# Stacking transfers of units 1 to 4 issued from two queues in turn

## The chip, the cores and the metric

The kernel runs on one core of a Trainium2 chip. The metric is the device time of one execution in microseconds (us). The core's engines are TensorE (PE; its weight loads are listed apart as PEld), VectorE (DVE), ScalarE (ACT), GpSimd (POOL) and SyncE (SP). Each executes its own instructions in order and waits on semaphores for the others. SyncE and ScalarE issue the transfers, which 16 DMA engines carry out.

## The reference

A linear recurrence with a complex diagonal decay per batch, head and key channel, followed by a bilinear feed-forward. Shapes: batch 4, 8 heads, 768 tokens, head width 48; the feed-forward is 384 to 1536 to 384.

```python
mag = sqrt(a_re*a_re + a_im*a_im)
scale = minimum(mag, 0.999) / (mag + 1e-6)
ar, ai = a_re*scale, a_im*scale                       # decay of each channel d at each token
for t in range(768):                                  # S_re, S_im: 48 x 48 per batch and head
    S_re, S_im = (ar[t]*S_re - ai[t]*S_im + outer(k[t], v[t]),
                  ar[t]*S_im + ai[t]*S_re)
    y[t] = q[t] @ S_re
x = y with the heads side by side                     # 3072 x 384
out = ((x @ w_a) * (x @ w_b)) @ w_out                 # 3072 x 384
```

## The kernel before

The work is cut into 12 **units** (`NU`): two pairs of batches, six chunks of 128 tokens each, so a unit covers 256 tokens (`TOK`, two batches of 128) for all eight heads. Three kinds of work run beside each other:

- **Prep** of a unit (`prep`, mostly VectorE with ScalarE): from the decays it forms running products z over the chunk, and multiplies queries and keys in the tile `qk` by them (L312 is the last of it, two multiplies for each unit from the third on, four for units 0 and 1, which are treated in two halves). Its first steps are the two multiplies of L214, the negation L216 on ScalarE, and then pairs of L230 and L236 on VectorE. Inside the prep of unit u runs `scale` for unit u+1 (L181 to L196), which turns raw decays into scale factors on ScalarE and VectorE.
- **Attention** of a unit (`attn`, mostly TensorE): scores by head (L385), a mask multiply on VectorE (L388), outputs (L425), transposes of the keys (L396, copied by ScalarE in L400) and the state update (L442). ScalarE (L429) and VectorE (L434) turn its result into the pair `xh`, `xl`.
- **Feed-forward** of a unit: twelve blocks f, each with `gemm1` (18 matmuls, L494), a copy and a product by ScalarE and VectorE (L502 to L505), and `gemm2` (6 matmuls, L512), which runs two blocks behind. ScalarE copies the two results of a unit (L651) and issues their transfers to memory (L652).

Between prep and attention stands the **stacking**. `qk` holds query and key rows of all heads in three groups of 128 partitions, and the tile `stk` holds, for each head, 96 partitions in which real and imaginary rows are stacked. `stack(u)` moves the one to the other by transfers from SBUF to SBUF: one for each head, two for heads 2 and 5, whose rows cross a group's border, so ten in all (L352). In the kernel before, SyncE issues all of them. For units 0 and 1 (`u < EARLY`) the first half of the columns is stacked earlier, in the middle of prep, by a call with explicit columns; the later call moves the other half.

The main loop goes over units w. While the feed-forward of unit w runs, the attention of unit w+1 is laid between its blocks, and prep for later units goes on. In the program text, at block 11 (10 for later w), the rest of the attention and of prep(w+2) is followed by stack(w+2), by the load of the next `qk` (L340, SyncE), and then by prep(w+3). For w = 0, stack(1) comes at block 4, in the middle of the conversion of the weights (L137 to L152), and is followed by eight extra matmuls (L681).

The order of instructions on each engine is set by a planner when the kernel is built: it goes through the program with its own estimate of every instruction's time, and at each moment takes for an engine the ready instruction that comes first in the program text. Some instructions are given a priority far ahead of their place (`high_priority`: the copies and products of the feed-forward, and the attention's steps on VectorE and ScalarE). From w+1 = 5 (`LED`) on, TensorE's order is the program's own, and the planner orders the other engines alone. On the chip, the engines then follow these orders, whatever the times.

Of the kernel before, what the change touches and what calls it, by code (L numbers as in the profile page):

```python
# [49 lines left out]
LED = 5  # L50
# [20 lines left out]
def tile_kernel(ctx: ExitStack, tc: tile.TileContext, a_d, qk_d, v_d, w_d, qn_d, kn_d, vn_d, an_d, out_d):  # L71
    nc = tc.nc
    vec, act, pe, sync = nc.vector, nc.scalar, nc.tensor, nc.sync
# [35 lines left out]
    stk = const.tile([128, H, RUN], F32, name="stk")  # L109
    nc.gpsimd.memset(stk[KS:128], 0.0)  # L110
    qk = const.tile([128, NJ, 2, RUN], F32, name="qk")
# [88 lines left out]
    def rescaled(c):  # L200
        return c % 2 == 1 and c + 1 < NCH

    def prep(u):
# [113 lines left out]
        if u < EARLY:  # L317
            for k in range(2):
                times_p(k, 0, 1)
            stack(u, slice(0, TOK))  # L320
# [20 lines left out]

    def stack(u, cols=None):
        n = RUN if rescaled(u % NCH) else 2 * TOK
        if cols is None:
            cols = slice(TOK if u < EARLY else 0, n)
        for h in range(H):
            r0 = h * D
            while r0 < (h + 1) * D:
                j, p = divmod(r0, 128)
                m = min((h + 1) * D - r0, 128 - p)  # L350
                d0 = 2 * (r0 - h * D)
                sync.dma_start(out=stk[d0:d0 + 2 * m, h, cols], in_=qk[p:p + m, j, :, cols])  # L352
                r0 += m


# [276 lines left out]
    drain(scale(0, a_tiles[0], z_first))  # L632
    drain(prep(0))
    stack(0)
    load_qk(1)
    p1 = prep(1)
# [19 lines left out]
    for w in range(NU):  # L656
# [15 lines left out]
        for f in range(NF):  # L672
            if w == 0:
                next(ws, None)
                drain(p1, P1_F)
                if f == P1_AT:
                    drain(p1)
                    stack(1)
                    for i in range(WARM):
                        wp = ps_m.tile([128, 512], F32, name="pm")  # L680
                        pe.matmul(out=wp[:, 0:TOK], lhsT=ident, rhs=qk[:, i % NJ, 1 - i // NJ % 2, TOK:2 * TOK],  # L681
                                  start=True, stop=True)
                    load_qk(2)
                    pgen = prep(2)
            pend.append((w, f, *gemm1(f, *x_cur), os_))
            if len(pend) > LAG:
                second()
            slot()
            if f == STACK_AT[min(w, 4)]:
                drain(at)  # L690
                if w + 2 < NU:
                    drain(pgen)
                    stack(w + 2)
                if w + 3 < NU:
                    load_qk(w + 3)
                    pgen = prep(w + 3)
            if w > 0:
                drain(pgen, 2400)
# [71 lines left out]
```

## Time and profile before

| | |
|---|---|
| median of 3 runs | 691.67 us (690.39 to 691.81) |
| profiled execution | 692.08 us |
| its span, first to last instruction | 690.4 us |
| mean granted TensorE clock | 0.974 |
| busy: PE, PEld | 647.5 us (94%), 607.9 us (88%) |
| busy: DVE, ACT | 552.1 us (80%), 306.7 us (44%) |
| stacking transfers | 140, of 32 to 193 KB |

The median and the profiled execution are two different readings: a trace explains its own execution. A row of the trace in order of time gives the start from the span's beginning, the length, engine, line of the kernel, operation, what it writes and reads, and in brackets the idle time of its engine just before and what ended it. SPq and ACTq are the queues of SyncE and ScalarE issuing transfers: such a row's length is that of the issue, not of the transfer; the landing is told apart. Rows of the same kind that follow each other are merged, with their count.

### The profile page before, as it was taken

What the parts mean: (1) busy time and instruction counts of PE and PEld (TensorE: products, weight loads), DVE (VectorE), ACT (ScalarE), POOL (GpSimd) and SP (SyncE); (2) the same over time, 40 slices, a digit from 0 to 9 for tenths busy, and PEclk for the clock granted to TensorE, in tenths of its full rate; (3) what the DMA queues carried; (4) which work ended last, traced back from release to release, by engine and by line L of the source; (5) the groups of instructions that cost most, each with busy time, mean ns of one, the idle gap of its engine ahead of it and who ended that gap; (6) DMA issues with size and microseconds to landing.
All of it is one profiled execution on the core that took longest, in us unless ns stands there. A gap on an engine that the chain in (4) does not pass through costs nothing.

```text
span 690.4 us, 14307 instructions
## 1 busy us (share of the span) xinstructions
PE 647.5 (94%) x5854; PEld 607.9 (88%) x5854; DVE 552.1 (80%) x1241; ACT 306.7 (44%) x618; POOL 5.6 (1%) x11
## 2 busy tenths in 40 slices
PE   3647999999999999999999999999999999999996
PEld 1224889899899999999999999999999999999995
DVE  6999899998898979989899898999989963233221
ACT  6347655634634445245353463634542332222221
POOL 3000000000000000000000000000000000000000
PEclk9577999999999999999999999999999999999999
DMA  8983201411414205224151250511410410400000
GB/s 310 402 303 109 80 1 47 139 54 49 137 43 125 87 28 150 62 92 131 32 161 47 84 155 1 166 73 49 121 69 16 112 65 18 107 24 2 24 1 28
DMA packets 32087, 63.93 MB, mean 93 GB/s; under 512 B 3984, under 2 KB 10640, under 8 KB 32016
## 3 DMA queue, kind: packets, MB, share of 16 engines
q1 hardware_dynamic: 28560, 58.23, 27.2%
q10 hardware_dynamic: 3456, 4.72, 1.9%
q8 instruction: 48, 0.79, 0.5%
q14 instruction: 23, 0.19, 0.1%
HBM read 39.32 MB, written 4.72 MB: 64 GB/s over the span
## 4 chain that ended last, share of the span: by engine, by line
PE 59%; DVE 31%; ACT 4%; DMA 2%; issue 2%; SPq 0%; ACTq 0%; DVEq 0%
PE ab L494 28%; PE o L512 13%; PE pm L385 5%; PE xp L425 4%; DVE a_t L292 3%; DVE qk L312 3%; PE pm L442 3%; DVE pr L230 2%; DVE hl L505 2%; DVE h_t L503 2%; PE pm L150 2%; DVE z L297 2%; DVE pb L260 2%; DVE z L236 1%; PE ab L150 1%
## 5 line engine op out<-in xcount | busy, mean ns | idle before, releaser
L494 PE MATMUL ab<-xh,w 128*128 128x256 f32 x1728 | 339.5, 285 | 0.0
L494 PEld LDWEIGHTS ab<-xh,w 128*128 128x128 f32 x1728 | 278.0, 190 | 1.0 <-issue 0.6
L494 PE MATMUL ab<-xl,w 128*128 128x256 f32 x864 | 245.1, 284 | 0.2 <-DVE xl L434 0.2
L494 PEld LDWEIGHTS ab<-xl,w 128*128 128x128 f32 x864 | 164.5, 190 | 1.0 <-DVE xl L434 0.7
L512 PE MATMUL o<-w,hh 128*128 128x384 f32 x576 | 149.5, 338 | 0.5 <-ACT o_sb L651 0.5
L502 ACT COPY h_t<-ab 128x256 f32<-128x256 f32 x144 | 53.3, 370 | 164.0 <-PE ab L494 163.0
L503 DVE TENSOR_TENSOR h_t<-ab,h_t 128x256 f32<-128x256 f32 x144 | 60.7, 421 | 64.8 <-ACT h_t L502 64.5
L504 ACT CAST hh<-h_t 128x256 fp32r<-128x256 f32 x144 | 58.2, 404 | 100.4 <-DVE h_t L503 100.0
L512 PEld LDWEIGHTS o<-w,hh 128*128 128x128 f32 x576 | 97.2, 190 | 1.7 <-ACT o_sb L651 1.1
L512 PE MATMUL o<-w,hl 128*128 128x384 f32 x288 | 97.0, 337 | 0.0
L505 DVE TENSOR_TENSOR hl<-h_t,hh 128x256 fp32r<-128x256 f32 x144 | 60.9, 423 | 21.5 <-ACT hh L504 21.3
L150 PE MATMUL ab<-o_sb,ident 128*128 128x384 f32 x42 | 27.8, 765 | 31.2 <-DVE o_sb L141 31.2
L385 PE MATMUL pm<-stk 128*128 128x128 f32 x384 | 53.5, 280 | 2.2 <-DMA stk<-qk 2.2
L512 PEld LDWEIGHTS o<-w,hl 128*128 128x128 f32 x288 | 54.1, 188 | 0.0
L385 PEld LDWEIGHTS pm<-stk 128*128 128x128 f32 x384 | 47.9, 191 | 6.9 <-issue 5.2
L230 DVE TENSOR_TENSOR pr<-z 128x384 f32<-128x384 f32 (+1 forms) x91 | 47.3, 527 | 2.7 <-ACT z L216 0.9
L150 PEld LDWEIGHTS ab<-o_sb,ident 128*128 128x128 f32 x42 | 10.0, 281 | 40.8 <-DVE o_sb L141 31.0
L292 DVE TENSOR_TENSOR a_t<-z,b_t 128x768 f32<-128x768 f32 x48 | 44.9, 956 | 0.0
L312 DVE TENSOR_TENSOR qk<-qk,z 128x1536 f32<-128x1536 f32 (+1 forms) x28 | 42.7, 1524 | 0.0
L425 PE MATMUL xp<-am,v_t 128*32 128x128 f32 x768 | 39.7, 276 | 0.7 <-DVE am L388 0.6
L388 DVE TENSOR_TENSOR am<-pm,mask 128x512 f32<-128x512 f32 x48 | 32.9, 689 | 4.0 <-PE pm L385 4.0
L425 PE MATMUL xp<-stk,u 128*32 128x128 f32 x640 | 32.7, 273 | 0.0
(106 smaller groups left out, 751.9 us busy)
## 6 DMA issues: line engine op xcount, KB each, us to landing
w<-in_dram SPq DMA_DIRECT2D x36, 384.0 KB, 8.0
qk<-in_dram SPq DMA_DIRECT2D x12, 768.0 KB, 4.9
a_t<-in_dram SPq DMA_DIRECT2D x11, 768.0 KB, 4.3
stk<-qk SPq DMA_DIRECT2D x42, 192.0 KB, 3.3
v_t<-in_dram SPq DMA_DIRECT2D x24, 256.0 KB, 2.7
out_dram<-o_sb ACTq DMA_DIRECT2D x24, 192.0 KB, 2.2
stk<-qk SPq DMA_DIRECT2D x18, 192.8 KB, 3.2
stk<-qk SPq DMA_DIRECT2D x14, 128.0 KB, 3.1
```

Of the source, the lines that this page charges most:

```text
L150: pe.matmul(out=lp[:, 0:n], lhsT=ident, rhs=t, start=True, stop=False)
L230: vec.tensor_tensor(out=pr[:, :, :, o:o + n], in0=view(zz, W + at_(i) + 2 * o, [[W, 2], [-W, 2], [2, n]]), in1=tok(slice(1, 3), i - 1, o, ...
L292: vec.tensor_tensor(out=pz[:, s].rearrange("p (j b e) -> p j b e", j=SUB // 2, e=2), in0=zb[:, 1 + s], in1=view(bb, (1 + k - s) * NB, [[0, ...
L312: vec.tensor_tensor(out=qk4[:, :, k, x0:x1], in0=qk4[:, :, 1, x0:x1], in1=z[:, k].rearrange("p (j t) -> p j t", j=NJ).unsqueeze(2).broadca ...
L385: pe.matmul(out=sp[:, h4], lhsT=stk[:, h, ks], rhs=stk[:, h, qs], start=True, stop=True)
L425: pe.matmul(out=xp[qd * 32:(qd + 1) * 32, ti], lhsT=l, rhs=rr, start=st, stop=sp_, tile_position=(0, qd * 32), skip_group_check=True)
L494: pe.matmul(out=ab[:, m * TOK:(m + 1) * TOK], lhsT=r(w_ab(f, part, m * NJ + i)), rhs=r(xt[:, i, :]), start=n == 0, stop=n == 8)
L502: act.copy(out=h_t, in_=ab[:, 0:TOK])
L503: vec.tensor_tensor(out=h_t, in0=ab[:, TOK:2 * TOK], in1=h_t, op=ALU.mult)
L504: act.copy(out=r(hh), in_=h_t)
L505: vec.tensor_tensor(out=r(hl), in0=h_t, in1=hh, op=ALU.subtract)
L512: pe.matmul(out=os_[tt][:, 0:DM], lhsT=r(ht[:, ts]), rhs=r(w_t[f, 2][:, part, :]), start=(f == 0 and n == 0), stop=(f == NF - 1 and n == 2))
```

## The change

`stack` gets a list of queues. For the call without explicit columns, and for units 1 to 4 (`0 < u < LED`), the list is SyncE and ScalarE, and the ten transfers are issued by them in turn: SyncE takes the first, third and so on, ScalarE the second, fourth and so on. For all other units, and for the early halves of units 0 and 1, SyncE issues all of them as before. The transfers themselves are the same.

```diff
     def stack(u, cols=None):
         n = RUN if rescaled(u % NCH) else 2 * TOK
+        queues = [sync]
         if cols is None:
             cols = slice(TOK if u < EARLY else 0, n)
+            if 0 < u < LED:
+                queues = [sync, act]
+        k = 0
         for h in range(H):
             r0 = h * D
             while r0 < (h + 1) * D:
                 j, p = divmod(r0, 128)
                 m = min((h + 1) * D - r0, 128 - p)
                 d0 = 2 * (r0 - h * D)
-                sync.dma_start(out=stk[d0:d0 + 2 * m, h, cols], in_=qk[p:p + m, j, :, cols])
+                queues[k % len(queues)].dma_start(out=stk[d0:d0 + 2 * m, h, cols], in_=qk[p:p + m, j, :, cols])
+                k += 1
                 r0 += m
```

## The prediction

> **What bounds the kernel now.** I read the page first, then busy time by stage, then the chain of work that ended last, and last the order of time around each stacking. The page gives the span; the profiled execution took 692.08 us in all, so 1.68 us lie around the span, and the median of the runs is 691.67 us, 0.41 us below this execution. A difference worked out inside the span is therefore added to 691.67.
>
> ```profile
> span 690.4 us, 14307 instructions
> ```
>
> Busy time by stretch (microseconds of the stretch, then busy time of PE, PEld, DVE, ACT):
>
> ```profile
> 85.00:170.00 85.00, 84.94 (x695) 78.33 (x694) 80.10 (x187) 43.65 (x90) 0.00 (x0) 1.00 0.19 55
> 170.00:262.00 92.00, 89.58 (x896) 85.75 (x895) 80.98 (x182) 43.26 (x82) 0.00 (x0) 1.00 0.28 85
> 262.00:391.00 129.00, 129.00 (x1254) 125.87 (x1253) 119.14 (x257) 61.24 (x119) 0.00 (x0) 1.00 0.31 91
> 391.00:556.00 165.00, 164.45 (x1592) 160.86 (x1591) 153.58 (x344) 75.86 (x151) 0.00 (x0) 1.00 0.31 93
> ```
>
> From 85 to 556 us TensorE is busy throughout, at a granted clock of 1.00, but for 2.4 us in the second row and 0.55 in the last. The second row holds the stackings of units 2 and 3. The chain there runs through the first stacking transfer of each unit to the score matmuls:
>
> ```profile
> 171.17 3.29 DMA stk<-qk
> ...
> 217.76 3.36 DMA stk<-qk
> ```
>
> TensorE in order of time (start, length, idle time before it and its releaser) shows the first scores of units 1 to 5 and its one later wait:
>
> ```profile
> 128.76 0.38 PE L385 MATMUL pm<-stk 128*128 128x128 f32 x2
> 174.59 0.46 PE L385 MATMUL pm<-stk 128*128 128x128 f32 x2 [1.57 <-DMA stk<-qk]
> 221.25 0.46 PE L385 MATMUL pm<-stk 128*128 128x128 f32 x2 [0.68 <-DMA stk<-qk]
> 268.69 0.85 PE L385 MATMUL pm<-stk 128*128 128x128 f32 x4
> 322.46 1.95 PE L385 MATMUL pm<-stk 128*128 128x128 f32 x16
> 555.46 0.61 PE L512 MATMUL o<-w,hh 128*128 128x384 f32 x2 [0.55 <-ACT o_sb L651]
> ```
>
> Units 2 and 3 stall TensorE for 1.57 and 0.68 us, together 2.25 us, each time for the **first** of the ten transfers and for none of the other nine. That sum is all that this change can take out of TensorE's path.
>
> **The change part by part.** Each of the four stackings has ten transfers (eight heads, of which heads 2 and 5 are cut in two). Of these five stay with SyncE and five go to ScalarE: 20 issues moved, nothing added or removed.
>
> *What the second queue saves.* SyncE's rows of units 1 to 5, each with ten issues:
>
> ```profile
> 122.32 6.34 SPq L352 DMA_DIRECT2D stk<-qk  x10
> 171.17 6.63 SPq L352 DMA_DIRECT2D stk<-qk  x10
> 217.76 6.67 SPq L352 DMA_DIRECT2D stk<-qk  x10
> 265.09 6.67 SPq L352 DMA_DIRECT2D stk<-qk  x10
> 308.88 6.67 SPq L352 DMA_DIRECT2D stk<-qk  x10
> ```
>
> Ten issues in 6.3 to 6.7 us are 0.64 to 0.67 us each with the gap. With five on each engine the issuing ends after 3.3 us instead of 6.7, if the two engines issue side by side. The data don't follow at that pace. For unit 3 the whole burst, and four microseconds in its middle (the last two numbers are the busy share of the 16 DMA engines and GB/s):
>
> ```profile
> 217.80:227.20 9.40, 8.72 (x69) 8.30 (x68) 8.36 (x18) 7.15 (x13) 0.00 (x0) 1.00 0.63 168
> 221.00:225.00 4.00, 3.75 (x30) 3.78 (x31) 3.03 (x7) 2.64 (x6) 0.00 (x0) 1.00 0.81 220
> ```
>
> The burst is 9.40 x 0.63 = 5.9 us of work for all 16 engines, and in its middle they are 81% busy already. A whole head is an eighth of that, 0.74 us. The first lands after 3.36 us, so its data start to move about 2.6 us after the issue, and the last can't land before 2.6 + 5.9 = 8.5 us, against 9.4 now: **0.9 us earlier for the last head, nothing for the first**. The first may land later, as the neighbour's packets now run beside its own: between 0 and 0.74 us late. [...]
>
> [...]
>
> For the stall this means: unit 2's 1.57 becomes 1.92. Unit 3's first transfer lands 0.35 later too, but TensorE also arrives 0.35 later, so the loss isn't counted twice. Unit 4 has its first transfer at 265.09 + about 3.3 = 268.4, and TensorE took it at 268.69: 0.3 us of cover, about enough. Unit 1 is transferred from 122.32 on and half its heads' columns were moved earlier; its scores start at 128.76, 6.4 us after the first issue, so its faster landing is worth nothing. **Term one: +0.35 us.** The load of `qk` behind the stacking on SyncE's queue may go out 0.9 us earlier; none of the waits shown above is for it, so it is costed at nothing.
>
> *What the issues cost on ScalarE.* ScalarE executes in order, and a DMA issue holds back what follows. The trace shows it at its own output transfers, and shows what stands where unit 2's five issues will go (171.2 us on):
>
> ```profile
> 204.63 0.34 ACTq L652 DMA_DIRECT2D out_dram<-o_sb  x1
> 205.01 0.41 ACT L504 CAST hh<-h_t 128x256 fp32r<-128x256 f32 x1 [0.41 <-ACT o_sb L651]
> ...
> 171.51 0.41 ACT L504 CAST hh<-h_t 128x256 fp32r<-128x256 f32 x1 [2.08 <-DVE h_t L503]
> 172.38 0.85 ACT L216 ACTIVATE z<-z 128x768 f32<-128x768 f32 x1 [0.46 <-DVE z L214]
> ...
> 126.74 0.85 ACT L216 ACTIVATE z<-z 128x768 f32<-128x768 f32 x1 [0.82 <-DVE z L214]
> ```
>
> At 205 us the cast waited 0.41 us through a 0.34 us issue. A stacking issue has another shape; its nearest row is SyncE's 0.64 us, and five of them are 3.2 us (bounds: 5 x 0.34 = 1.7 and 5 x 0.67 = 3.4; I take 3.2, because the transfers are the very same). In the program text stack(u) comes before prep(u+1), so the planner has reason to put the issues ahead of L216, the negation that opens the next unit's scan, and of L181 after it; the high-priority cast L504 can slip between. L216 then starts at 171.17 + 3.2 + 0.41 = 174.8 at the latest, and 172.38 at the best (issues behind it). VectorE needs it:
>
> ```profile
> 173.85 0.55 DVE L230 TENSOR_TENSOR pr<-z 128x384 f32<-128x384 f32 x1
> ...
> 178.24 0.69 DVE L388 TENSOR_TENSOR am<-pm,mask 128x512 f32<-128x512 f32 x1 [0.78 <-PE pm L385]
> 182.85 0.69 DVE L388 TENSOR_TENSOR am<-pm,mask 128x512 f32<-128x512 f32 x1 [0.53 <-PE pm L385]
> 189.12 0.42 DVE L503 TENSOR_TENSOR h_t<-ab,h_t 128x256 f32<-128x256 f32 x1 [0.90 <-ACT h_t L502]
> ```
>
> L230 would start at 174.8 + 0.85 = 175.7 instead of 173.85: up to 1.8 us late, 0 at best. Behind it VectorE has idle time of 0.78 + 0.53 + 0.90 = 2.2 us before 190 us that could swallow this, but each of those waits is for TensorE, and a mask multiply L388 that comes late on VectorE's queue makes TensorE late in turn. So the net is between 0 and 1.8 us for a unit; I take the middle, 0.9 minus a bit for L504 and L502 that fill part of the hole: **0.8 us**. It counts where the next stacking is waited for: after unit 2 (unit 3's stall) and after unit 3 (unit 4, less its 0.3 us of cover). After unit 4 it doesn't count: unit 5's transfers are issued from 308.88 and its scores come at 322.46, 13.6 us later, against 9.4 us that a burst takes. After unit 1 it doesn't either: L216 comes at 126.74, and the five issues end at 122.32 + 3.2 = 125.5.
>
> **The sum.** TensorE is 0.35 us late after unit 2. Unit 3's data come 0.35 + 0.8 late: 1.15. Unit 4's come 0.35 + 1.6 late with 0.3 covered: 1.65. Past 262 us TensorE has no idle time, so that stays; the 0.55 at 555 us gives no cover, since the chain into it is itself fed by TensorE:
>
> ```profile
> 386.70 0.42 DVE L503 TENSOR_TENSOR h_t<-ab,h_t 128x256 f32<-128x256 f32 x1 [0.93 <-ACT h_t L502]
> ```
>
> Here VectorE waits for a gemm result by way of ScalarE. 692.08 + 1.65 = 693.7 us against the profiled execution, **693.3 us** against the median. Its own range is 692.0 (only term one is left) to 695.3 (1.8 for each of the two units, less 0.3, plus 0.35).
>
> **The rivals.**
>
> *Absorbed.* VectorE's 2.2 us of idle time swallow the late L216, and only term one is left: 691.67 + 0.35 = 692.0 us. For it speaks that those waits really are idle; against it that they end with TensorE's own work.
>
> *Faster: the new plan pulls the scores later.* TensorE's order for units 1 to 4 is the planner's, and it placed unit 2's first score 1.57 us too early. If the planner prices the issues on ScalarE dear, it puts VectorE's chain and the scores later against the gemms; the chip then finds the data landed, and both stalls vanish: 2.25 us. From then on the gain must get past 386.70, where VectorE's idle time for TensorE is 0.93 us, and 555.46, where TensorE already waits 0.55 us for the ScalarE and VectorE chain; so 0.93 is the lower bound of what is kept and 2.25 the upper. With 1.7, nearer the upper bound because that chain has other waits, 690.0 us. It decides as soon as the scores move back by more than L216's lateness.
>
> *Slower still: the two issue streams wait for each other.* At unit 6 two output transfers from ScalarE fell into SyncE's burst. The stacking issues of unit 3 and of unit 6 (min/median/max ns, then us to landing), and all of ScalarE's issues:
>
> ```profile
> L352 SPq DMA_DIRECT2D stk<-qk x10: 585/600/722, 217.8 to 223.8; - x10
> DMA to landing us min/median/max: 2.6/3.2/3.4
> L352 SPq DMA_DIRECT2D stk<-qk x10: 576/596/1596, 351.9 to 359.7; - x10
> DMA to landing us min/median/max: 2.6/3.2/4.8
> L652 ACTq DMA_DIRECT2D out_dram<-o_sb x24: 338/338/473, 151.2 to 684.7; - x24
> ```
>
> The longest issue grew from 722 to 1596 ns and the longest landing from 3.4 to 4.8 us. If the streams take turns, the change doesn't do what it says: nothing is issued sooner, and ScalarE is held for all ten issues, 6.4 us. L216 then starts at 171.17 + 6.4 + 0.41 = 178.0 and L230 at 178.85, 5.0 us late; with 2.2 swallowed that is 2.8 for each of the two units, and 5.6 - 0.3 + 0.35 = 5.65 in all: 697.3 us. It decides as soon as ScalarE's issues take clearly more than 0.64 us each. Against it: the neighbours at unit 6 wrote to HBM, and no issue of ScalarE's took over 473 ns.
>
> [...]
>
> **How the numbers follow.** A measurement of this kernel tells 0.2% from no change, 1.38 us. Chances: the forecast 0.42 (two thirds of it, 0.28, beyond +1.38 us), absorbed 0.20, faster 0.24 (0.22 beyond -1.38 us), slower still 0.14. Slower is 0.28 + 0.14 = 0.42, same 0.14 + 0.20 + 0.02 = 0.36, faster 0.22. The range runs from 689.9 us, 1.8 of the faster rival's 2.25 us, to 697.0 us, just short of the last rival; it leaves out about half of that one and the end of the other.
>
> **What would show it.** Right: ten transfers on two queues with issues side by side, the first landing after 3.3 to 4.1 us, the last some 8.5 us after the first issue; L216 of units 2 to 4 starting two microseconds later against L312's end; VectorE's idle time before L230 up; TensorE's waits for `stk` at units 2 and 3 at or above 1.6 and 0.7 us. Wrong: those waits gone while L216 stays in place, or issues on ScalarE of 0.34 us, or a TensorE wait in a stage past 262 us, where I expect none.

## The result, and the profile after

The changed kernel takes **705.23 us** (median of four runs, 700.73 to 705.85) against 691.52 us for the kernel before (four runs): a ratio of 1.0183, 95% interval 1.0167 to 1.0199, or 13.7 us more. The prediction was 693.3 us. The profiled execution took 705.57 us. One of the four runs, 700.73 us, had a mean granted clock of 0.972 where the others had 0.965 or 0.966; it left no trace. In the rows of the changed kernel the lines of the program have moved down: the stacking L352 is L356, and from there on all stand five further, the scores L385 at L390, the mask multiply L388 at L393, the first gemm L494 at L499, the feed-forward's copy L502 and product L503 at L507 and L508; L214 to L312 are where they were.

The page's span, and busy time by stretch of the changed kernel (same columns and stretches as in the prediction):

```profile
span 703.9 us, 14315 instructions
```

```profile
85.00:170.00 85.00, 84.00 (x688) 77.21 (x687) 79.08 (x185) 42.81 (x89) 0.00 (x0) 1.00 0.18 51
170.00:262.00 92.00, 85.80 (x840) 81.42 (x839) 74.53 (x170) 37.21 (x72) 0.00 (x0) 0.96 0.29 84
262.00:391.00 129.00, 125.05 (x1166) 121.12 (x1165) 111.38 (x233) 61.52 (x116) 0.00 (x0) 0.99 0.31 92
391.00:556.00 165.00, 165.00 (x1634) 161.56 (x1633) 153.62 (x341) 76.27 (x154) 0.00 (x0) 1.00 0.27 78
```

TensorE is idle for 1.00 + 6.20 + 3.95 + 0 = 11.15 us of these 471, where it was 3.03 before: 8.1 us more. And its granted clock, 1.00 everywhere before, is 0.96 over 92 us and 0.99 over 129, about 5 us of full speed. Together that is 13.1 of the 13.5 us by which the span grew. So there are two losses to explain, waits and a lower clock, and the second stood in no case of the prediction.

The waits, in TensorE's order of time, for units 2, 3, 4 and 5 of the changed kernel:

```profile
175.43 0.46 PE L390 MATMUL pm<-stk 128*128 128x128 f32 x2 [1.74 <-DMA stk<-qk]
176.97 0.49 PE L390 MATMUL pm<-stk 128*128 128x128 f32 x2 [1.08 <-DMA stk<-qk]
...
179.42 0.80 PE L390 MATMUL pm<-stk 128*128 128x128 f32 x2 [0.46 <-DMA stk<-qk]
...
227.31 0.46 PE L390 MATMUL pm<-stk 128*128 128x128 f32 x2 [1.28 <-DMA stk<-qk]
229.22 0.79 PE L390 MATMUL pm<-stk 128*128 128x128 f32 x2 [1.45 <-DMA stk<-qk]
...
280.66 0.46 PE L390 MATMUL pm<-stk 128*128 128x128 f32 x2 [0.66 <-DMA stk<-qk]
282.47 0.49 PE L390 MATMUL pm<-stk 128*128 128x128 f32 x2 [1.34 <-DMA stk<-qk]
...
337.63 0.83 PE L390 MATMUL pm<-stk 128*128 128x128 f32 x4 [1.10 <-DMA stk<-qk]
```

Before, TensorE waited once in unit 2 and once in unit 3, for the first head, and not at all in units 4 and 5. Now it waits for the **second** head too, by 1.08, 1.45 and 1.34 us, in unit 4 as well, and by 1.10 us even in unit 5, which SyncE stacks alone as before.

ScalarE in order of time at unit 2, and VectorE behind it:

```profile
171.83 0.60 ACTq L356 DMA_DIRECT2D stk<-qk  x1
172.48 0.41 ACT L509 CAST hh<-h_t 128x256 fp32r<-128x256 f32 x1 [2.39 <-DVE h_t L508]
172.50 1.32 ACTq L356 DMA_DIRECT2D stk<-qk  x1
...
173.95 0.85 ACTq L356 DMA_DIRECT2D stk<-qk  x1
...
177.03 1.24 ACTq L356 DMA_DIRECT2D stk<-qk  x2
178.32 0.84 ACT L216 ACTIVATE z<-z 128x768 f32<-128x768 f32 x1 [3.07 <-DMA stk<-qk]
```

```profile
175.28 0.42 DVE L510 TENSOR_TENSOR hl<-h_t,hh 128x256 fp32r<-128x256 f32 x1 [0.53 <-ACT hh L509]
180.26 0.69 DVE L393 TENSOR_TENSOR am<-pm,mask 128x512 f32<-128x512 f32 x1 [4.55 <-PE pm L390]
180.86 0.55 DVE L230 TENSOR_TENSOR pr<-z 128x384 f32<-128x384 f32 x1
```

The five issues reach from 171.83 to 178.27, 6.4 us, and L216 comes at 178.32 (172.38 before). Between 174.80 and 177.03 ScalarE issues nothing: but for a cast of 0.40 us it waits, and the row of L216 names the landing of a stacking transfer. (The 3.07 us in that row are this wait, from 175.24 on, and the two issues behind it.) The order of ScalarE's instructions as the planner wrote it, with the semaphores that each waits for, shows what for (DMAHW0 to 7 are the eight semaphores on which the transfers of both queues report that they have landed):

```
192 L356 DMA stk<-qk 96x1x512 [waits DMAHW2_49]
193 L509 CAST hh<-h_t 128x256 [waits DVE_49]
194 L356 DMA stk<-qk 64x1x512 [waits DMAHW5_49,DMAHW4_49,DMAHW1_49]
195 L356 DMA stk<-qk 96x1x512 [waits DMAHW6_49]
196 L216 ACTIVATE z<-z 128x768
```

With one queue an issue waits for the transfer eight places ahead, which had landed by then: in unit 2 the first transfer landed at 174.46 and the ninth was issued at 176.55, and SyncE's ten issues of before follow each other within 6.63 us, without a pause. With two, ScalarE's fourth issue waits for transfers that are under way, its own first one among them (DMAHW5), issued 5.2 us earlier and landed at 176.93.

VectorE, for its part, did not wait for L216 in unit 2. It waited 4.55 us for a score, since its new order has the mask multiply L393 ahead of the next unit's L230; before, L230 ran at 173.85, ahead of the mask multiply at 178.24. The two delays lie over each other: L216 ended at 179.16, so even ahead of the mask multiply L230 could have begun only 1.7 us earlier. In unit 3 the held ScalarE shows on VectorE directly. There the feed-forward's copy L507 stood behind a landing wait of ScalarE's issues, and VectorE's product L508 behind the copy:

```profile
230.96 0.37 ACT L507 COPY h_t<-ab 128x256 f32<-128x256 f32 x1 [4.90 <-DMA stk<-qk]
```

```profile
231.37 0.42 DVE L508 TENSOR_TENSOR h_t<-ab,h_t 128x256 f32<-128x256 f32 x1 [4.85 <-ACT h_t L507]
```

Between 165 and 345 us its mask multiplies, before and after, had these waits (busy time and mean ns of one, then the idle time before them and what ended it):

```profile
L388 DVE TENSOR_TENSOR am<-pm,mask 128x512 f32<-128x512 f32 x16 | 11.1, 691 | 2.2 <-PE pm L385 2.2
```

```profile
L393 DVE TENSOR_TENSOR am<-pm,mask 128x512 f32<-128x512 f32 x14 | 9.6, 688 | 13.2 <-PE pm L390 13.2
```

The planner wrote all three orders anew. TensorE's, around unit 2 (h0: the scores of head 0; g5: five feed-forward matmuls), as it was executed:

```
before:  h0 g5 h1 g11 h2 g4 h3 g4 h4
after:   h0 h1 g5 h2 g2 h3 g3 h4
```

The planner now lays heads 0 and 1 directly behind each other, as if two queues delivered two heads at a time. The chip delivered otherwise: TensorE started head 0 at 175.43 and head 1 at 176.97. The stacking transfers of unit 2, before and after (issue time min/median/max in ns, then us from issue to landing):

```profile
L352 SPq DMA_DIRECT2D stk<-qk x10: 592/599/718, 171.2 to 177.2; - x10
...
DMA to landing us min/median/max: 3.0/3.7/4.8
```

```profile
L356 SPq DMA_DIRECT2D stk<-qk x5: 595/767/904, 171.8 to 174.9; - x5
L356 ACTq DMA_DIRECT2D stk<-qk x5: 588/608/1324, 171.8 to 177.7; - x5
...
DMA to landing us min/median/max: 3.5/4.9/6.3
```

A transfer took 1.2 us longer at the median. TensorE could start head 1 at 176.97, 5.15 us after the first issue.

The clock, in two neighbouring stretches of 3.41 us at unit 2 (the column behind POOL's busy time is the granted clock):

```profile
174.56:177.97 3.41, 1.46 (x10) 1.29 (x11) 0.62 (x2) 0.40 (x1) 0.00 (x0) 1.00 0.98 252
177.97:181.38 3.41, 2.95 (x15) 2.66 (x14) 1.12 (x2) 2.31 (x3) 0.00 (x0) 0.50 0.55 129
```

After a stretch in which TensorE was idle for 1.95 of 3.41 us, it ran one stretch at half its clock. The same follows the waits of units 3 and 4, at 229.17 and 283.79 us. A stretch of 3.41 us at half clock does 1.7 us less work: three times 1.7 us.

### The profile page after: what moved, and what is told of

It reads as the page before. It is cut to its first block, busy times and chain, and to the rows that moved or that the text cites. A ratio compares the mean times of both kernels' runs of the same rounds, so it can differ in the third digit from the quotient of the medians.

```text
span 703.9 us, 14315 instructions
## 1 busy us (share of the span) xinstructions
PE 654.8 (93%) x5854; PEld 612.2 (87%) x5854; DVE 551.1 (78%) x1241; ACT 307.3 (44%) x618; POOL 5.6 (1%) x11
## 4 chain that ended last, share of the span: by engine, by line
PE 66%; DVE 19%; DMA 7%; ACT 3%; SPq 3%; issue 1%; ACTq 0%; DVEq 0%
PE ab L499 32%; PE o L517 15%; PE pm L390 6%; PE xp L430 5%; DMA stk<-qk 4%; PE pm L447 3%; DMA w<-in_dram 3%; DVE qk L312 3%; DVE a_t L292 3%; SPq L356 3%; PE pm L401 2%; DVE h_t L508 1%; DVE z L297 1%; DVE hl L510 1%; DVE pb L260 1%
## 5 line engine op out<-in xcount | busy, mean ns | idle before, releaser
L499 PE MATMUL ab<-xh,w 128*128 128x256 f32 x1728 | 341.1, 286 | 0.0
L499 PEld LDWEIGHTS ab<-xh,w 128*128 128x128 f32 x1728 | 279.5, 191 | 1.0 <-issue 0.6
L499 PE MATMUL ab<-xl,w 128*128 128x256 f32 x864 | 245.9, 285 | 0.2 <-DVE xl L439 0.2
L499 PEld LDWEIGHTS ab<-xl,w 128*128 128x128 f32 x864 | 165.3, 191 | 0.8 <-DVE xl L439 0.5
L507 ACT COPY h_t<-ab 128x256 f32<-128x256 f32 x144 | 53.0, 368 | 165.3 <-PE ab L499 159.3
L508 DVE TENSOR_TENSOR h_t<-ab,h_t 128x256 f32<-128x256 f32 x144 | 60.5, 420 | 65.5 <-ACT h_t L507 65.1
L390 PE MATMUL pm<-stk 128*128 128x128 f32 x384 | 56.3, 289 | 9.9 <-DMA stk<-qk 9.9
L390 PEld LDWEIGHTS pm<-stk 128*128 128x128 f32 x384 | 49.6, 196 | 16.4 <-issue 8.5
L230 DVE TENSOR_TENSOR pr<-z 128x384 f32<-128x384 f32 (+1 forms) x91 | 47.3, 527 | 2.8 <-ACT z L216 1.1
L393 DVE TENSOR_TENSOR am<-pm,mask 128x512 f32<-128x512 f32 x48 | 32.7, 687 | 14.9 <-PE pm L390 14.9
L312 DVE TENSOR_TENSOR qk<-qk,z 128x1536 f32<-128x1536 f32 (+1 forms) x28 | 42.7, 1523 | 0.2
```

What stands on the lines that cost most here:

```text
L230: vec.tensor_tensor(out=pr[:, :, :, o:o + n], in0=view(zz, W + at_(i) + 2 * o, [[W, 2], [-W, 2], [2, n]]), in1=tok(slice(1, 3), i - 1, o, ...
L312: vec.tensor_tensor(out=qk4[:, :, k, x0:x1], in0=qk4[:, :, 1, x0:x1], in1=z[:, k].rearrange("p (j t) -> p j t", j=NJ).unsqueeze(2).broadca ...
L390: pe.matmul(out=sp[:, h4], lhsT=stk[:, h, ks], rhs=stk[:, h, qs], start=True, stop=True)
L499: pe.matmul(out=ab[:, m * TOK:(m + 1) * TOK], lhsT=r(w_ab(f, part, m * NJ + i)), rhs=r(xt[:, i, :]), start=n == 0, stop=n == 8)
L507: act.copy(out=h_t, in_=ab[:, 0:TOK])
L508: vec.tensor_tensor(out=h_t, in0=ab[:, TOK:2 * TOK], in1=h_t, op=ALU.mult)
```

## The experiments

Three suspects came out of this: **the chip** (colliding transfers), **ScalarE** (held by its issues), and **the plan** (new orders on three engines). Each run gives its median, the difference from the kernel before on the same chip and, in brackets, the 95% interval of the ratio. The program's text is the same but for the edit shown; where lines of it are left out there stands "...".

**Only ScalarE issues** (units 1 to 4).

```diff
-                queues = [sync, act]
+                queues = [act]
```

> ScalarE issues all ten transfers of units 1 to 4, SyncE none of them. There is one queue, so no sharing, and ScalarE is held for twice as many issues. Theory A: L216 comes 6.5 us or more late, and the time is above that of the changed kernel: 706 to 715 us. Theory B: the heads land 3.3, 4.1, 4.6 us after the first issue as before the change, and the time is 691 to 695 us.

720.94 us, +29.2 (ratio 1.0396 to 1.0444), more than either theory said. No transfers of two queues collide here (the median stacking transfer of unit 2 takes 3.0 us from issue to landing), and the loss doubles. The lateness is handed on: at unit 5, which SyncE stacks again, TensorE waits for the first head for 9.10 us. The granted clock is 0.50 for 20.5 us in all, 10.2 of the 29.2 us. The planner's orders are new here too.

```profile
344.90 2.03 PE L390 MATMUL pm<-stk 128*128 128x128 f32 x6 [9.10 <-DMA stk<-qk]
```

**GpSimd instead of ScalarE.**

```diff
-                queues = [sync, act]
+                queues = [sync, nc.gpsimd]
```

> Units 1 to 4 stack from SyncE and GpSimd in turn, so ScalarE issues nothing, while the two queues still share the 16 DMA engines. Theory A (ScalarE is held by its issues; L216, L507 and so VectorE's chain come late): L216 comes back to within 1 us of its place before and the time to 691 to 694 us. Theory B (the second and later heads land later when two queues share the DMA engines, and TensorE waits for each): the second head still lands about 5.1 us after the first issue of unit 2 against 4.07 before, TensorE still waits for heads in the middle of the burst, and at least two thirds of the loss stays: 701 to 706 us.

706.35 us, +14.6 (1.0173 to 1.0230). ScalarE issues nothing, and L216 is at its place (172.15); the loss is all there. So the held ScalarE isn't needed for a loss of this size. But GpSimd isn't a clean stand-in: it too made the planner write new orders, under which VectorE waits 17.7 us for scores between 165 and 345 us, and 8.5 us of the loss are stretches at half clock.

**Tiny transfers on ScalarE, all data from SyncE.**

```diff
...
-                queues[k % len(queues)].dma_start(out=stk[d0:d0 + 2 * m, h, cols], in_=qk[p:p + m, j, :, cols])
+                sync.dma_start(out=stk[d0:d0 + 2 * m, h, cols], in_=qk[p:p + m, j, :, cols])
+                if len(queues) > 1 and k % 2:
+                    act.dma_start(out=scr[d0:d0 + 2 * m, k, :], in_=qk[p:p + m, j, :, 2 * TOK - 2:2 * TOK])
```

> SyncE issues all ten transfers as before the change; ScalarE issues, in the five places that it had, transfers of 8 bytes a row to a tile that nothing reads. Theory A: ScalarE is held as in the changed kernel (five issues and their waits, up to 6.4 us), and the time is 702 to 706 us. Theory B: the second head lands about 4.1 us after the first issue as before the change, and the time is 691 to 694 us. If both are needed it lies between, near 698 us.

695.68 us, +3.9 (1.0035 to 1.0079), between the two. ScalarE was held for less long, with L216 at 175.65, 3.3 us late instead of 5.9, and the data were not left as before either: SyncE's ten issues took 8.27 us instead of 6.63. Neither theory alone fits these first three runs.

**Unit 2 alone from two queues.**

```diff
-            if 0 < u < LED:
+            if u == 2:
```

> Only unit 2 is stacked from two queues. If each unit pays for itself (a quarter of 13.7 us, whichever theory), 695 us; if the loss is a lateness that is handed on from unit to unit and grows, 692 to 693 us here, with the stacking of unit 3 issued 0 to 2 us later than before; if one unit is enough to upset all that follows, over 700 us.

696.83 us, +5.0 (1.0036 to 1.0078): one unit pays for itself, and more than a quarter. The stacking of unit 3 is issued at 223.50, 5.7 us later than before, where I had expected 2 at most; without a second queue in the units behind it this lateness hardly grows (6.4 us at unit 5). TensorE's rows show 1.79 us of wait for head 0 and 1.57 for head 1, and the granted clock is 0.50 for 6.83 us behind them, 3.4 us of the 5.0:

```profile
174.36 0.46 PE L390 MATMUL pm<-stk 128*128 128x128 f32 x2 [1.79 <-DMA stk<-qk]
...
176.40 0.80 PE L390 MATMUL pm<-stk 128*128 128x128 f32 x2 [1.57 <-DMA stk<-qk]
```

```profile
175.04:181.87 6.83, 5.47 (x25) 5.30 (x25) 2.07 (x4) 2.31 (x3) 0.00 (x0) 0.50 0.55 136
```

To part the plan from the chip, the next runs impose an engine's order as another kernel has it, written down as a list and tied by edges that order the issue and make nothing wait:

```diff
+    def pin(engine, n, order):
...
+        for a, b in zip(seq, seq[1:]):
+            tc.add_manual_dep(ins[b], ins[a].name, mybir.DependencyInfo(mybir.DependencyClass.NoSync,
+                              mybir.DependencyReason.DATA), reason="pin")
...
+    pin(pe.engine, 4753, ORDER_PE)
```

**Two queues, TensorE's order of before.**

> Two queues as in the changed kernel, but TensorE's order is that of the kernel before, written down and imposed (the planner orders the other engines around it). The traces show that the planner, when it is told of two queues, lays heads 0 and 1 of a unit directly behind each other and only 5, 2 and 3 feed-forward matmuls between the next ones, where before it had laid 5, 11, 4 and 4. Theory P (the plan: TensorE's order expects the heads in pairs and in half the time, and the chip doesn't deliver them so): with the old order back, most of the loss goes, 692 to 696 us. Theory Q (the chip: two queues that collide, and a ScalarE that is held, whatever the order): 701 to 706 us.

706.04 us, +14.4 (1.0186 to 1.0246): nothing is won. My first form of the plan theory, that TensorE's pairs of heads are the cause, falls. The waits are there (1.76 and 0.85 us at unit 2), and so are ScalarE's hold and VectorE's early mask multiplies, since the planner fits those orders around TensorE's: between 165 and 345 us VectorE waits 7.9 us for L216 and 7.5 for scores.

**Two queues, all three orders of before.**

> Two queues, with the orders of TensorE, VectorE and ScalarE (without its transfers) all imposed as they were in the kernel before; only ScalarE's twenty issues are put between by the planner, ahead of L216. Theory P: 692 to 696 us, with what is left due to the held ScalarE alone (3.9 us in the run with the tiny transfers). Theory Q: 701 to 706 us. If this run is below the one with TensorE's order alone, the planner's order of VectorE and ScalarE had its own share.

701.10 us, +9.5 (1.0125 to 1.0187). That is what the two queues cost by themselves, with no new plan. VectorE now waits 0.4 us for scores in units 2 to 4 instead of 13.2, but L216 stands behind the issues in these orders too. It comes 4.90 to 4.93 us after the first issue of its stacking in units 2 to 4, where it was 1.20 to 1.54 us before. In ScalarE's group between 165 and 345 us, columns as above, the idle time holds the issues and the landing waits between them:

```profile
L216 ACT ACTIVATE z<-z 128x768 f32<-128x768 f32 x4 | 3.4, 846 | 12.4 <-DMA stk<-qk 11.6 <-DVE z L214 0.9
```

**One queue, TensorE's order of after.**

> One queue (the transfers of the kernel before), with TensorE's order of the changed kernel imposed. Theory P: the second head lands 4.0 us after the first issue, TensorE has no work laid between, and waits of 0.3 to 1 us at the second and later heads come back without any second queue: 698 to 705 us. Theory Q: 691 to 693 us.

694.07 us, +2.4 (1.0023 to 1.0051), between the two cases: TensorE's new order alone costs little. Its one dear place is the clock: here heads 0 and 1 came behind a wait of 1.62 us for head 0, against 1.57 in the kernel before, and 3.41 us at half clock followed.

**One queue, all three orders of after.**

> One queue, with the orders of TensorE, VectorE and ScalarE all as in the changed kernel, less ScalarE's issues. Theory P: 698 to 705 us, no less than with TensorE's order alone. Theory Q: 691 to 693 us.

701.30 us, +9.7 (1.0116 to 1.0159). So the plan costs 9.7 us without any second queue, and 7.2 of them (9.66 less 2.43) lie with VectorE's and ScalarE's orders. Two stretches at half clock, 3.4 us, are in it. VectorE at unit 2, and its group of mask multiplies between 165 and 345 us:

```profile
174.16 0.43 DVE L505 TENSOR_TENSOR hl<-h_t,hh 128x256 fp32r<-128x256 f32 x1 [0.47 <-ACT hh L504]
177.78 0.69 DVE L388 TENSOR_TENSOR am<-pm,mask 128x512 f32<-128x512 f32 x1 [3.20 <-PE pm L385]
178.39 0.55 DVE L230 TENSOR_TENSOR pr<-z 128x384 f32<-128x384 f32 x1
```

```profile
L388 DVE TENSOR_TENSOR am<-pm,mask 128x512 f32<-128x512 f32 x15 | 10.3, 689 | 11.4 <-PE pm L385 11.4
```

**One queue, VectorE's order alone of after.**

> One queue; VectorE's order alone is that of the changed kernel, the planner orders the others around it. If VectorE's mask multiplies L388, standing early in its order, are the cause of the 9.7 us that the changed kernel's orders cost by themselves: 697 to 702 us, with VectorE idle for L385 at 8 us or more between 165 and 345 us (2.2 us in the kernel before). If the other orders are as much to blame: 691 to 695 us.

705.11 us, +13.4 (1.0165 to 1.0212), above the range of its first case, with VectorE idle for scores for 17.2 us; 3.4 us of the loss are at half clock. The mask multiply ahead of L230 is enough: VectorE stands still with the next unit's prep behind it. It is more than with all three orders; that the other two, which the planner fitted around it, suit it less is likely, but no run shows it. There is no time for VectorE's new order beside the old orders of TensorE and ScalarE: put together, the three would wait for each other in a circle.

```profile
L388 DVE TENSOR_TENSOR am<-pm,mask 128x512 f32<-128x512 f32 x14 | 9.5, 687 | 17.2 <-PE pm L385 17.2
```

**The sharing alone: GpSimd as second queue, all three orders of before.**

> The two queues are SyncE and GpSimd, and TensorE, VectorE and ScalarE run in the orders of the kernel before. What is left is the sharing of the DMA engines alone: no planner's new order, nothing issued on ScalarE. If that sharing makes the larger part of the 9.5 us that two queues cost under the old orders (701.1 us with ScalarE as the second queue): 698 to 703 us. If the held ScalarE makes it: 692 to 695 us, with L216 back at its place.

697.82 us, +6.0 (1.0072 to 1.0103). ScalarE is free and the plan is old, and heads that land late still hold VectorE at its mask multiplies, 9.3 us in units 2 to 4. Two stretches at half clock (3.4 us) are in it. The result lies just below the range that I gave to the sharing as the larger part. It isn't the share of the collisions in the run with ScalarE: with GpSimd the median transfer of unit 2 took 6.2 us from issue to landing, under the same orders with ScalarE 4.7.

```profile
L393 DVE TENSOR_TENSOR am<-pm,mask 128x512 f32<-128x512 f32 x16 | 11.1, 691 | 9.3 <-PE pm L390 9.3
```

**Tiny transfers under the orders of before.**

> SyncE moves all the data; ScalarE issues five transfers of 8 bytes a row; all three orders are those of the kernel before. What is left is ScalarE's hold alone. If the hold makes the larger part of the 9.5 us: 696 to 700 us, with L216 3 to 5 us late. If the sharing makes it: 692 to 694 us.

698.67 us, +6.8 (1.0089 to 1.0120), and not clean: the tiny transfers use the same eight landing semaphores, and SyncE's own ten issues took 9.23 us instead of 6.63, so the data came late too. Hence the next run, with no transfer more.

**ScalarE held by copies, one queue, all three orders of before.** The copies read `qk` when its stacking is issued and write a tile that nothing reads.

```diff
...
+        if 1 < u < LED and cols == slice(0, n):
+            for _ in range(17):
+                last_of[u] = act.activation(out=scr, in_=qk[:, 2, 1, 0:64], func=AF.Copy, scale=-1.0).ins.name
...
```

> One queue, all three orders of the kernel before; in units 2 to 4 ScalarE executes 17 copies of 128x64 ahead of L216, about 3.4 us by an estimate of 0.2 us each, which stand for the time that its five issues hold it, with no second queue and no transfer more. If a held ScalarE by itself costs about what the run with the tiny transfers under the same orders did (6.9 us, but there SyncE's fourth issue came 1.6 us late as well): 696 to 699 us. If ScalarE's and VectorE's idle time takes it up: 692 to 693.5 us.

703.24 us, +11.5 (1.0153 to 1.0187), more than either guess. Seventeen copies took 0.55 + 4.29 = 4.8 us, more than the 3.4 they were meant for (257 ns each at the mean, where I had guessed 0.2 us), and L216 came 4.95 us after the first issue of its stacking in each of the three units (176.67 against 171.72 in unit 2): 3.4 to 3.75 us later than before. What that does, on VectorE and then on TensorE at unit 2 (in this kernel L512 and L513 are the feed-forward's copy and product, L398 the mask multiply, L406 the transposes):

```profile
177.78 0.42 DVE L513 TENSOR_TENSOR h_t<-ab,h_t 128x256 f32<-128x256 f32 x1 [3.69 <-ACT h_t L512]
```

```profile
182.38 0.55 PE L406 MATMUL pm<-ident,stk 96*128 96x96 f32 x4 [2.48 <-DVE am L398]
```

VectorE waited 3.69 us, and not for L216 but for the feed-forward's copy L512, which stands behind it on ScalarE (in unit 4 it waited 3.10 us for L216 itself). The mask multiply came late, and TensorE's transposes, which need the place in PSUM that it frees, waited 2.48 us. Over three units: 11.5 us for 10.9 us of hold, about 1 for 1. Two stretches at half clock, 3.4 us, are in it.

By luck the copies hold L216 as long as two queues do under these same orders (4.95 us after the first issue, against 4.90 to 4.93), and there VectorE waits for the copy in the same way:

```profile
176.61 0.42 DVE L508 TENSOR_TENSOR h_t<-ab,h_t 128x256 f32<-128x256 f32 x1 [3.65 <-ACT h_t L507]
```

So under the old orders a hold of ScalarE, with no second queue, is enough for all that the two queues cost (+11.5 against +9.5).

**Three issues on ScalarE instead of five.**

```diff
-                queues[k % len(queues)].dma_start(out=stk[d0:d0 + 2 * m, h, cols], in_=qk[p:p + m, j, :, cols])
+                queues[k % len(queues) if k < 6 else 0].dma_start(out=stk[d0:d0 + 2 * m, h, cols], in_=qk[p:p + m, j, :, cols])
```

> ScalarE issues only the second, fourth and sixth transfer, SyncE the other seven, in the planner's own orders. ScalarE's fourth and fifth issue in the changed kernel waited for earlier transfers to land (L216 waited 3.07 us behind them), so without those two it should be free about 3 us sooner: L216 at 2 to 3.5 us after its place of before, instead of 6. The planner lays heads 0 and 1 of a unit together, then 8, 2, 6 and 3 feed-forward matmuls. If the waits of ScalarE's last two issues make most of the loss: 694 to 698 us; if the early collisions and the planner's order do: 701 to 705 us.

702.14 us, +10.4 (1.0141 to 1.0175). L216 came at 175.35, 3 us after its place of before, as foreseen, and 3.1 us of the loss went; the second heads still land late (TensorE waits 1.35 us at unit 2) and three stretches at half clock are there. The last two issues with their landing wait are a part, not the bulk.

**The changed kernel with TensorE kept busy.** All three orders of after, and matmuls laid into the waits.

```diff
...
+            busy = {0: 3, 1: 4} if 1 < u < LED and (i, hg) == (0, 0) else {}
...
             for h4 in range(4):
                 h = hg * 4 + h4
+                for _ in range(busy.get(h4, 0)):
+                    e = pe.matmul(out=sp[:, h4], lhsT=ident, rhs=ident, start=True, stop=True).ins
...
```

> The changed kernel, with all three of its orders imposed as they are, and 7 matmuls more in each of units 2 to 4, which multiply the identity by itself into a place that the next score overwrites: 3 ahead of the first score, 4 ahead of the second. They stand where TensorE waited, about 0.7 and 0.9 us of work, and take nothing from the waits' ends. The trace of the changed kernel shows the granted clock at 0.50 for three stretches of 3.41 us right after such waits, which is 1.7 us each. If the idle time brings the clock down: the three stretches are gone and the time is 700 to 702 us. If the clock falls for another reason: 705 to 706.5 us.

**700.48 us**, +8.8 (1.0117 to 1.0151): 21 matmuls that compute nothing made the changed kernel 4.75 us faster; all four runs lie between 699.55 and 701.23 us, where three of the changed kernel's four lie above 704.8. The same two stretches as above, in this kernel:

```profile
174.56:177.97 3.41, 2.27 (x17) 2.08 (x18) 0.59 (x2) 0.40 (x1) 0.00 (x0) 1.00 0.98 243
177.97:181.38 3.41, 2.86 (x23) 2.23 (x21) 2.02 (x4) 2.68 (x4) 0.00 (x0) 1.00 0.60 135
```

No stretch at half clock is left between 85 and 556 us, where the granted clock is 1.00 throughout. The lower clock was 4.75 of the 13.7 us by this run; the three stretches of the trace come to 5.1.

**The other way to fill the stall: the kernel before, with feed-forward matmuls laid ahead of the scores.**

> One queue and the orders of the kernel before, but 13 more feed-forward matmuls laid ahead of unit 2's first score and 12 ahead of unit 3's (taken from behind the same unit's scores), so that TensorE has work in the 1.57 and 0.68 us that it waits there. If those two waits are all that the stacking costs: 689.0 to 690.5 us. If VectorE's chain sets the pace behind them, the wait only moves to the next unit: 691 to 693 us.

691.27 us, ratio 0.9989 (0.9980 to 0.9998; 11 runs against 15): 0.6 us faster, not to be told from no change by the bound of 0.2%. So the second case came true. The waits for the first heads are gone, and others took their place, among them these on TensorE:

```profile
178.58 0.46 PE L385 MATMUL pm<-stk 128*128 128x128 f32 x2 [0.45 <-DMA stk<-qk]
182.58 0.60 PE L385 MATMUL pm<-stk 128*128 128x128 f32 x3 [0.57 <-ACT kt L400]
```

In sum, as differences from the kernel before:

| | one queue | two queues |
|---|---|---|
| all orders of before | 0 | +9.5 |
| TensorE's order alone of after, or of before | +2.4 (after) | +14.4 (before) |
| all orders of after | +9.7 | +13.7 |
| ... and TensorE kept busy | | +8.8 |

Stretches at half clock are in these numbers, by the one trace of each run: 5.1 us in +13.7, 3.4 in +9.7 and in +14.4, 1.7 in +2.4, none in +9.5 (whose trace is of the fastest of its four runs, 699.45 to 704.50 us) and none in +8.8.

The plan and the queues each cost nearly 10 us, and together 13.7, not 19. Each makes the same chain late (scores, mask multiplies, VectorE's prep, the next unit's stacking), and VectorE waits for what comes last. How the 13.7 would divide between them therefore has no single answer. Under the old orders a hold of ScalarE alone reaches the queues' part; under the new ones no run parts the hold from the late second heads.

## Why the prediction was wrong, point by point

The direction was right, and for reasons that the prediction named: the first transfer isn't faster, and ScalarE's hold costs more than the queue saves. The size was wrong by a factor of eight, and the time lies 8 us above the range. By its steps:

- **"Nothing for the first" head, 0.35 us late: right, and small.** No run shows the 0.35 us themselves, my half of a bound of 0.74; what the runs showed in their place is 0.2. In units 2 and 3 the first head's scores start 3.61 and 3.69 us after the first issue instead of 3.42 and 3.49. TensorE's wait for it went from 1.57 to 1.74 us in unit 2; I had said 1.92.
- **"0.9 us earlier for the last head", and no word on the heads between: wrong.** I shared the DMA engines for the first transfer only and left the second at its old landing. The median transfer took 4.9 us instead of 3.7, and the second head's wait, 1.08, 1.45 and 1.34 us in units 2 to 4, is larger than the whole of my term one.
- **Five issues hold ScalarE for 3.2 us: mis-sized, 6.4 us.** I counted issues by their length and not what each waits for. Two things were missing: an issue beside one of the other queue grew to 1.32 us, and the last two come only after a landing wait, at 177.03. The rival "slower still" put L216 at 178.0, and it came at 178.32, but not for its reason, and its time, 697.3 us, is still 8 us short. The streams didn't take strict turns: the first issues ran side by side, in 0.60 us each, though ScalarE's second took 1.32.
- **A hold of 3.2 us nets 0.8 us for a unit: the step that failed most.** I let VectorE's idle time swallow it and followed L216 alone. The run with copies shows about 1 us lost for 1 us of hold, by way of the feed-forward's copy that queues behind it. One of the three waits on VectorE that I counted as cover, 0.90 us at 189.12, was a wait for that very copy. I had written that a late mask multiply "makes TensorE late in turn", and then priced it at a quarter.
- **Unit 1 at nothing, unit 4 at half a microsecond: wrong.** TensorE lost 0.9 us at unit 1 (84.00 busy against 84.94 by 170 us), where it waited 0.94 us for the weight conversion L145, which stood behind ScalarE's issues; in unit 4 it waited 0.66 and 1.34 us, though I had counted on 0.3 us of cover.
- **TensorE's order was taken as fixed.** I allowed for a new plan only as a rival for the better (scores later). The plan went the other way on all three engines, and alone costs 9.7 us. Where the mask multiplies stand is decided by the planner's estimates and not by the chip; that its estimate of the landings moved them is likely, but not shown.
- **The clock was left at 1.00.** 4.75 us by the run with TensorE kept busy: a third of the loss.
- **No wait past 262 us: wrong,** as I had named among the signs against me. Unit 5 shows 1.10 us at 337.63; the first issues of units 3, 4 and 5, at 217.76, 265.09 and 308.88 us before, come at 223.62, 277.20 and 328.99:

```profile
171.82 3.95 SPq L356 DMA_DIRECT2D stk<-qk  x5
223.62 4.40 SPq L356 DMA_DIRECT2D stk<-qk  x5
277.20 4.25 SPq L356 DMA_DIRECT2D stk<-qk  x5
328.99 7.42 SPq L356 DMA_DIRECT2D stk<-qk  x10
```

The lateness of VectorE's chain grows by 5 to 8 us with each unit, until TensorE has no cover left.

## What to carry to other kernels

Moving an issue to an engine that computes is to be priced by all that stands behind it on that engine, and by what the issue itself waits for; idle time elsewhere is no cover unless the waits there end with something else than the delayed work (here 10.9 us of hold cost 11.5 us). Where a planner orders the engines, a change of queues changes its picture of when data land: compare the two orders, around the change and on every engine, before pricing the change on the chip. And look at what short waits do to TensorE's clock: here 21 matmuls that compute nothing won 4.75 us.

## What the runs showed of the hardware

TensorE's clock fell after waits of one to two microseconds, which the prediction had not reckoned with. In the traces of this study the granted clock drops to 0.50, ahead of the end of the run, for 3.41 us at a time or a multiple of it, at instants that within one trace lie whole multiples of 3.41 us apart (177.97, 229.17 and 283.79 in the changed kernel: 15 and 16 steps). I divided each trace of the 17 kernels into such steps, in phase with its own stretches, between 85 and 400 us, and took those at full clock with at least 0.8 us of idle TensorE, 58 in all. All 16 with 1.85 us or more idle were followed by a step at half clock; of 32 below 1.6 us, 2 were; between, 4 of 10. The wait of the kernel before, 1.57 us in one step, lies just below that band, and the 1.62 us of the run with TensorE's order of after just inside it (start and length of the step, PE busy, ..., granted clock):

```profile
172.90:176.31 3.41, 1.84 (x15) 1.75 (x15) 3.34 (x7) 2.48 (x6) 0.00 (x0) 1.00 0.85 211
176.31:179.72 3.41, 3.41 (x35) 3.29 (x37) 2.56 (x7) 2.77 (x4) 0.00 (x0) 1.00 0.78 218
```

```profile
171.85:175.26 3.41, 1.79 (x13) 1.32 (x11) 3.34 (x7) 2.72 (x5) 0.00 (x0) 1.00 0.84 213
175.26:178.67 3.41, 3.41 (x17) 3.26 (x16) 2.86 (x7) 2.72 (x3) 0.00 (x0) 0.50 0.66 181
```

So idle time in about half of a step was enough: 1.62 us of 3.41 here, 1.95 in the changed kernel from 174.56 on.

In unit 2 of the changed kernel the two queues issue their first transfers side by side in 0.60 us each; the second takes 0.60 us on SyncE and 1.32 on ScalarE, the third 0.77 and 0.85. With GpSimd as the second queue ScalarE was spared, and the transfers still landed late (6.2 us at the median instead of 3.7, and +6.0 us under the old orders).
